# An attention and mixer kernel on one core: the first channel matmul of six groups by Strassen's scheme

## The chip, the core and the metric

The kernel runs on one core of one Trainium2 chip. Its engines run side by side, each with its own instruction queue: TensorE (PE, matrix products, with a separate record PEld for loading the stationary operand), VectorE (DVE), ScalarE (ACT), GpSimd (POOL), and SyncE (SP), which here only issues transfers (DMAs). The metric is the device time of one execution in microseconds (us), lower is better. Matrix products read from on-chip memory (SBUF) and add into banks of a second memory (PSUM), from which DVE and ACT read.

## What is computed

Linear attention on 8 x 8 heads of 576 rows and 64 columns, then an MLP mixer over the tokens and one over the channels, all in float32:

```python
q_s = softmax(q, axis=-1);  k_s = softmax(k, axis=2)
attn = einsum('bhsd,bhde->bhse', q_s, einsum('bhsd,bhse->bhde', k_s, v))
x = attn.transpose(0, 2, 1, 3).reshape(8, 576, 512)
h = relu(x.transpose(0, 2, 1) @ w_tok1) @ w_tok2      # 576 -> 256 -> 576
u = x + h.transpose(0, 2, 1)
out = u + relu(u @ w_ch1) @ w_ch2                     # 512 -> 1536 -> 512
```

The last line is where most of the arithmetic lies: 4608 rows by 512 by 1536, twice. `ch1` is the first of these products with its relu, `ch2` the second.

## The kernel before

**Precision.** A float32 operand is held as two tiles in a reduced float32 (F32R), a high part and the remainder (names ending in h and l; `split`, L108 and L109: ACT copies the high part, DVE or POOL subtracts for the remainder). A product is three matmuls: high by high, remainder of the weights by high, high by remainder of the data.

**Groups and steps.** The 4608 rows of `u`, transposed, are cut into nine groups of 512 columns, kept in three slots `uT[g]`, each of four blocks n of 128 channels. w_ch1 and w_ch2 are cut into twelve rows f of 128. A step (g, f) is `ch1(g, f)`, 4 blocks x 3 = 12 matmuls of 512 columns (L412) into one bank `ps_h`, then relu on ACT (L415, `h2h`) and the remainder on DVE (L416, `h2l`), and `ch2` of the step before (L427): 12 matmuls of 512 columns into four banks `ps_o` that gather over all f. At a group's end `out_end` adds the residual (L459) and sends the group out. The weights of ch1 and ch2 stay in SBUF: `c1h`, `c1l`, `c2`.

**The order.** The list `steps` runs group 0 for f below 4, group 1, the rest of group 0 (24 steps, n0 = 24), and then groups 2 to 8, twelve steps each. Between ch1 and ch2 of a step, functions from the list `todo` are called, which `put(step, function)` has filled: the attention units. A unit is two heads of one batch; batch b is worked on during group b - 1 and gives `uT` of group b (and the end of the group before). Its stages: softmax of q and k (`soft`, DVE, ACT, POOL), `stage_qT` (32x32 transposes on DVE, their copies L331), `stage_kv` (L283), `stage_y` (L345: 14 matmuls of 256 columns), `stage_h1` (L353), `stage_u` (L390), whose result goes to `uT` (L397, L398). `begin` issues the loads of a later unit on SP (`kt` L146, `q` L138, `k` L151; `v` L161 and L162 are issued in `stage_kv`). After the last step of group g POOL computes the residual `u` of its four blocks (`residual`, L442).

**What sets the order on each engine.** The program's order gives priorities; a planner that simulates the engines at compile time lays out each engine's queue (SP's too) by what is ready, and puts in the semaphores. On the chip every queue is then worked off in that order. `behind(...)` ties an instruction behind another on its engine.

**Banks.** `ps_h` has four banks, shared by ch1 and all attention stages from step 0 on; `ps_o` has four, for ch2.

**Weights.** In the first steps `load_ch` loads float64 weights, narrows them on DVE and ACT and splits them; rows 4 to 11 in steps 1 to 11.

Of the kernel before, what the change touches and what calls it, by code (L numbers as in the profile page):

```python
# [20 lines left out]
def attn_mixer_kernel(ctx: ExitStack, tc: tile.TileContext, q, k, kt, v, wt, out, dims):  # L21
# [25 lines left out]
    hpool = ctx.enter_context(tc.tile_pool(name="hpool", bufs=2))  # L47
# [55 lines left out]
    def f32(ap):  # L103
        return ap.bitcast(F32)

    def split(hi, lo, src, lo_eng):

        nc.scalar.copy(hi, src)  # L108
        lo_eng.tensor_tensor(lo, src, f32(hi), op=ALU.subtract)  # L109
# [55 lines left out]
    def load_weights(i, n=CW, out=None):  # L165

        if not wide:
            t = out if out is not None else cv.tile([P, C1 * P], F32, name="cv_s")[:, 0:n]
            nc.sync.dma_start(t, wt[i][:, 0:n])
            return t  # L170
        conv.append(conv.pop(0))
        raw = conv[-1][0].tile([P, CW, 2], U32, name="stg")
        nc.sync.dma_start(raw[:, 0:n, :].rearrange("p n w -> p (n w)"), wt[i][:, 0:n].bitcast(U32))
        with behind(first):
            return narrow(raw, n, out)
# [38 lines left out]
        split(w2h[:, :, S0:S], w2l[:, :, S0:S], t, nc.vector)  # L214

    def load_ch(f):
        h_, l_ = (w[:, f].rearrange("p n m -> p (n m)") for w in (c1h, c1l))
        split(h_, l_, load_weights(AT_C1 + f), nc.vector)
        split(*c2[f], load_weights(AT_C2 + f), nc.vector)

# [145 lines left out]
    uT = [slots[i] for i in (0, 1, 2, 1, 0, 2, 1, 0, 2)]  # L366
# [33 lines left out]


    drained = []

    def ch1(g, f):
        hh = hpool.tile([P, CW], F32R, name="h2h")
        hl = hpool.tile([P, CW], F32R, name="h2l")
        t = ps_h.tile([P, 512], F32, name="ps_h")
        i = 0
        for n in range(NJ):
            uh, ul = (x[:, n, :] for x in uT[g])  # L410
            for a, w in ((c1h, uh), (c1l, uh), (c1h, ul)):
                nc.tensor.matmul(t, a[:, f, n, :], w, start=(i == 0), stop=(i == 3 * NJ - 1))  # L412
                i += 1
        drained[:] = [
            nc.scalar.activation(hh, t, AF.Relu).ins,  # L415
            nc.vector.scalar_tensor_tensor(hl, t, 0.0, f32(hh), op0=ALU.max, op1=ALU.subtract).ins,  # L416
        ]
        return hh, hl

    def ch2(acc, f, first, last, hh, hl, in_turn=False):  # L420

        at = []
        for n, o in enumerate(acc):
            cs = slice(n * P, (n + 1) * P)
            for i, (a, w) in enumerate(((c2[f][0], hh), (c2[f][1], hh), (c2[f][0], hl))):
                with behind(at):
                    m = nc.tensor.matmul(o, a[:, cs], w, start=(first and i == 0), stop=(last and i == 2))  # L427
# [3 lines left out]
    def stage_rows():

        for n in range(0, NJ, 2):
            t = stg.tile([P, CW, 2], U32, name="stg").rearrange("p n w -> p (n w)").bitcast(F32)
            res[n], res[n + 1] = t[:, 0:CW], t[:, CW : 2 * CW]

    def residual(g):

        stage_rows()
        for n in range(NJ):  # L440
            uh, ul = (x[:, n, :] for x in uT[g])
            nc.gpsimd.tensor_tensor(res[n], f32(uh), f32(ul), op=ALU.add)  # L442

    res = {}

    def out_end(g, acc, whole):
        if g == 1:
            stage_rows()
        for n, o in enumerate(acc):
            uh, ul = (f32(x[:, n, :]) for x in uT[g])  # L450
            if g == NG - 1:

                for x, eng in ((slice(0, CW // 2), nc.scalar), (slice(CW // 2, CW), nc.sync)):
                    nc.vector.tensor_tensor(res[n][:, x], o[:, x], res[n][:, x], op=ALU.add)
                    eng.dma_start(out[g, n][:, x], res[n][:, x])
                continue
            if g > 1:
                t = res[n]
                nc.vector.tensor_tensor(t, o, t, op=ALU.add)  # L459
# [94 lines left out]
    steps = [(0, f) for f in range(F_HEAD)] + [(1, f) for f in range(NF)] + [(0, f) for f in range(F_HEAD, NF)]  # L554
    n0 = len(steps)
# [26 lines left out]
    pend = None  # L582

    load_at = dict(zip((1, 2, 4, 5, 7, 8, 10, 11), range(F_HEAD, NF)))
    for i, (g, f) in enumerate(steps):
        if i in load_at:
            if load_at[i] == F_MORE:
                more_pools.close()
                conv[:] = [(stg, cv)]
                c2_rows(F_MORE, NF)  # L590
            with behind(drained):
                load_ch(load_at[i])
        h = ch1(g, f)
# [9 lines left out]
        if pend is None or pend[0] != g:  # L603
            acc = [ps_o.tile([P, CW], F32, name="ps_o") for _ in range(NJ)]
        pend = (g, acc, f, pend is None or pend[0] != g, last, *h)
        if last and g > 1:
            residual(g)
    assert not todo

    ch2(*pend[1:], in_turn=True)  # L610
    out_end(*pend[:2], True)


def pieces(w_tok1, w_tok2, w_ch1, w_ch2):
# [53 lines left out]
```

## Time and profile before

| what | value |
|---|---|
| median of 3 runs | 824.63 us (824.05 to 824.95) |
| profiled execution, first to last instruction (its span) | 822.3 us |
| around the span, against the median | 2.3 us |
| DMA | 63.55 MB, mean 77 GB/s |
| ACT busy | 325.1 us |
| POOL busy | 113.2 us |

The profile is that of one execution. Busy times are sums over the span; a busy PE says that matmuls are in flight. A slice row gives, for each fortieth of the span, a digit that is the busy share in tenths. A stage row gives the busy time of each engine inside a window. A row of a group of instructions has the source line, the engine and operation, output and inputs by the program's names, shapes and count, then the busy time in us and the mean of one in ns, then the time that the engine stood idle before them, and for what.

### The profile page before, as it was taken

How to read it: one execution, taken by the hardware profiler on the slowest of the kernel's cores; microseconds unless marked ns; L12 is line 12 of the kernel's file. 1: busy time of each engine (PE TensorE's matmuls, PEld its weight loads, DVE VectorE, ACT ScalarE, POOL GpSimd, SP SyncE). 2: the span in 40 equal slices, each digit the busy share in tenths (PEclk: the TensorE clock that was granted, in tenths of full speed). 3: DMA queues.
4: the chain of work that ended last, by engine and by line, in shares of the span. 5: the costliest groups of instructions: out<-in, count | busy, mean ns of one | idle time of the engine just before them, and what ended most of it. 6: DMA issues, size and time to landing. Idle time of an engine off the chain costs nothing.

```text
span 822.3 us, 11725 instructions
## 1 busy us (share of the span) xinstructions
PE 796.0 (97%) x4464; PEld 669.9 (81%) x4464; DVE 496.9 (60%) x1080; ACT 325.1 (40%) x758; POOL 113.2 (14%) x93
## 2 busy tenths in 40 slices
PE   3799999999999999999999999999999999999998
PEld 2688888778888888888888888888888888888886
DVE  7999998999775555756657654655566322112112
ACT  4676543466543344434434443444434321111100
POOL 1000000022211011311122011311131102001100
PEclk9999999999999999999999999999999999999999
DMA  8653533424222122322232221322131001001001
GB/s 247 231 143 119 189 118 103 129 69 145 79 61 84 51 63 63 98 63 63 63 114 63 50 60 39 108 63 62 32 98 47 16 1 52 1 0 52 1 1 51
DMA packets 61208, 63.55 MB, mean 77 GB/s; under 512 B 40928, under 2 KB 42080, under 8 KB 61152
## 3 DMA queue, kind: packets, MB, share of 16 engines
q1 hardware_dynamic: 55968, 53.88, 22.3%
q10 hardware_dynamic: 5184, 8.92, 3.0%
q8 instruction: 35, 0.57, 0.3%
q14 instruction: 21, 0.17, 0.1%
HBM read 53.35 MB, written 9.44 MB: 76 GB/s over the span
## 4 chain that ended last, share of the span: by engine, by line
PE 82%; DVE 9%; DMA 4%; ACT 2%; issue 2%; POOL 0%; SPq 0%; ACTq 0%; DVEq 0%; POOLq 0%
PE ps_h L412 32%; PE ps_o L427 32%; PE ps_h L390 7%; PE ps_h L345 5%; PE ps_h L283 2%; DMA q_t<-in_q 2%; PE ps_h L353 1%; DVE q_t L331 1%; PE ps_o L390 1%; PE ps_h L242 1%; DMA out<-stg 1%; DVE h2l L416 1%; DVE st L252 1%; DVE q_t L253 1%; PE ps_o L345 1%
## 5 line engine op out<-in xcount | busy, mean ns | idle before, releaser
L416 DVE SCALAR_TENSOR_TENSOR h2l<-ps_h,h2h 128x512 fp32r<-128x512 f32 x108 | 74.1, 686 | 163.0 <-ACT h2h L415 162.4
L427 PE MATMUL ps_o<-h2h,c2h 128*128 128x512 f32 x432 | 169.2, 392 | 1.2 <-ACT h2h L415 1.2
L412 PE MATMUL ps_h<-uh,c1h 128*128 128x512 f32 x432 | 169.2, 392 | 0.0
L427 PE MATMUL ps_o<-h2h,c2l 128*128 128x512 f32 x432 | 168.8, 391 | 0.0
L412 PE MATMUL ps_h<-uh,c1l 128*128 128x512 f32 x432 | 168.7, 391 | 0.0
L412 PE MATMUL ps_h<-ul,c1h 128*128 128x512 f32 x432 | 168.6, 390 | 0.0
L415 ACT ACTIVATE h2h<-ps_h 128x512 fp32r<-128x512 f32 x108 | 64.5, 597 | 250.8 <-PE ps_h L412 233.0
L427 PE MATMUL ps_o<-h2l,c2h 128*128 128x512 f32 x432 | 152.6, 394 | 0.0
L331 DVE COPY q_t<-cv_s 32x160 f32<-32x160 f32 (+1 forms) x252 | 67.6, 268 | 61.6 <-POOL ql L109 58.5
L427 PEld LDWEIGHTS ps_o<-h2h,c2h 128*128 128x128 f32 x432 | 81.1, 188 | 18.1 <-ACT h2h L415 1.6
L412 PEld LDWEIGHTS ps_h<-ul,c1h 128*128 128x128 f32 x432 | 81.1, 188 | 17.4
L427 PEld LDWEIGHTS ps_o<-h2h,c2l 128*128 128x128 f32 x432 | 81.2, 188 | 16.2
L412 PEld LDWEIGHTS ps_h<-uh,c1h 128*128 128x128 f32 x432 | 81.1, 188 | 15.9
L412 PEld LDWEIGHTS ps_h<-uh,c1l 128*128 128x128 f32 x432 | 81.2, 188 | 15.0
L427 PEld LDWEIGHTS ps_o<-h2l,c2h 128*128 128x128 f32 x432 | 79.6, 188 | 15.8
L244 POOL TENSOR_TENSOR k_t<-k_t,dg 128x640 f32<-128x640 f32 x24 | 38.2, 1592 | 310.4 <-ACT dg L243 296.3
L109 POOL TENSOR_TENSOR ql<-q_t,qh 128x640 fp32r<-128x640 f32 x24 | 37.7, 1569 | 197.4 <-ACT qh L108 161.2
L442 POOL TENSOR_TENSOR stg<-uh,ul 128x512 f32<-128x512 f32 x28 | 35.5, 1290 | 141.3 <-DMA out<-stg 111.8
L252 DVE TENSOR_REDUCE st<-q_t 128x10 f32<-128x640 f32 x32 | 26.1, 816 | 37.0 <-DMA q_t<-in_q 36.8
L262 ACT ACTIVATE q_t<-q_t 128x640 f32<-128x640 f32 x32 | 23.6, 738 | 47.1 <-DVE q_t L253 47.0
L331 ACT COPY q_t<-cv_s 32x128 f32<-32x128 f32 (+1 forms) x132 | 40.6, 307 | 2.9 <-DVE cv_s L321 1.4
L390 PE MATMUL ps_h<-w2h,hh 128*128 128x256 f32 (+1 forms) x112 | 32.9, 301 | 0.1
(144 smaller groups left out, 1152.1 us busy)
## 6 DMA issues: line engine op xcount, KB each, us to landing
stg<-in_w SPq DMA_DIRECT2D x28, 512.0 KB, 3.4
kt_t<-in_kt SPq DMA_DIRECT2D x32, 320.0 KB, 2.9
q_t<-in_q SPq DMA_DIRECT2D x32, 320.0 KB, 2.9
v_t<-in_v SPq DMA_DIRECT2D x64, 128.0 KB, 3.0
k_t<-in_k SPq DMA_DIRECT2D x24, 320.0 KB, 3.5
out<-stg ACTq DMA_DIRECT2D x28, 256.0 KB, 3.4
v_t<-in_v SPq DMA_DIRECT2D x32, 32.0 KB, 2.9
out<-part ACTq DMA_DIRECT2D x4, 256.0 KB, 3.5
```

The costliest lines, as they stand in the source:

```text
L109: lo_eng.tensor_tensor(lo, src, f32(hi), op=ALU.subtract)
L244: nc.gpsimd.tensor_tensor(kx, kx, dg.unsqueeze(1).broadcast_to([P, C1, P]), op=ALU.subtract)
L252: nc.vector.tensor_reduce(st[:, 0, :], qt, axis=AX.X, op=ALU.max)
L262: nc.scalar.activation(qc, qc, AF.Exp)
L331: eng(qx[ys, 0:n, xs], turned[xs, 0:n, ys])
L345: nc.tensor.matmul(y[:, 0:TOK], a, w, start=(i == 0), stop=(i == len(mm) - 1))
L390: nc.tensor.matmul(t[:, 0:N], a, w, start=(i == 0), stop=(i == len(mm) - 1))
L412: nc.tensor.matmul(t, a[:, f, n, :], w, start=(i == 0), stop=(i == 3 * NJ - 1))
L415: nc.scalar.activation(hh, t, AF.Relu).ins,
L416: nc.vector.scalar_tensor_tensor(hl, t, 0.0, f32(hh), op0=ALU.max, op1=ALU.subtract).ins,
L427: m = nc.tensor.matmul(o, a[:, cs], w, start=(first and i == 0), stop=(last and i == 2))
L442: nc.gpsimd.tensor_tensor(res[n], f32(uh), f32(ul), op=ALU.add)
```

## The change

For groups 3 to 8 (from `G_S` = 3) two rows f of ch1 are computed together as a product of 2 x 2 blocks: weights A cut into (two rows f) x (two halves of the 512 channels), data B cut into (two halves of the channels) x (two halves of 256 columns). In the form of Strassen's scheme that uses 7 products, the products are

- P1 = A11 B11, P2 = A12 B21, P3 = (A12 - A21 - A22 + A11) B22, P4 = A22 (B21 - B22 + B12 - B11)
- P5 = (A21 + A22)(B12 - B11), P6 = (A21 + A22 - A11)(B22 - B12 + B11), P7 = (A11 - A21)(B22 - B12)

each of 2 blocks x 3 matmuls of 256 columns. The weight sums are made once per pair of rows (`keep_sums`), split, and written to memory with the plain blocks (`keep_blocks`), in steps 18 to 32. They come back product by product into a ring of eight SBUF tiles of 256 KB (`load_product`, on SP, issued when the tile's former product is done). The ring and the tiles of the data sums take the place of c1's rows, which are in two pools now and are closed in steps 32 and 35. The data sums are made once per group on DVE and split (`data_sums`); they need `u` as one float32 value per element, so the residual is made before the group (`row_sum`), three blocks on POOL and one on DVE. `pair_a` (P1, P6, P5, P7, in the even step) and `pair_b` (P2, P3, P4, in the odd step) join the products in SBUF, then come relu and remainder as before, from SBUF. A pair's two halves go to ch2 one per step, from the step after. Attention units of batches 3 to 7 start one step earlier. Groups 0 to 2 keep the old ch1.

```diff
+    h2 = hpool.tile([P, 2, 2, CW], F32R, name="h2")
     def ch1(g, f):
-        hh = hpool.tile([P, CW], F32R, name="h2h")
-        hl = hpool.tile([P, CW], F32R, name="h2l")
+        hh, hl = (h2[:, x, f % 2, :] for x in range(2))
...
+    def keep_blocks(p):
+        scratch_w[p] = [dpool.tile([P, 2, 2 * P], F32, name=f"w{p}_{i}") for i in range(7)]
+        for e, f, n in ((P1, 2 * p, 0), (P2, 2 * p, 2), (P4, 2 * p + 1, 2)):
+            for x, w in enumerate(c1_row(f)):
+                nc.sync.dma_start(scratch_w[p][e][:, x, :], f32(w[:, n : n + 2, :].rearrange("p n m -> p (n m)")))
+    def keep_sums(p):
...
+        nc.vector.tensor_tensor(a, f32(wh[:, i : i + 2]), f32(wl[:, i : i + 2]), op=ALU.add)
...
+        nc.vector.tensor_tensor(s[:, 0], a21, a22, op=ALU.add)
+        nc.vector.tensor_tensor(s[:, 1], s[:, 0], a11, op=ALU.subtract)
+        nc.vector.tensor_tensor(s[:, 2], a11, a21, op=ALU.subtract)
+        nc.vector.tensor_tensor(s[:, 3], a12, s[:, 1], op=ALU.subtract)
+        split(hi, lo, f32(lo), nc.vector)
+        for k, e in enumerate(sums):
+            for x, w in enumerate((hi, lo)):
+                nc.sync.dma_start(scratch_w[p][e][:, x, :], f32(w)[:, k * 2 * P : (k + 1) * 2 * P])
...
+    def load_product():
...
+            nc.sync.dma_start(f32(ring[i % 8].rearrange("p n m -> p (n m)")), scratch_w[p][e].rearrange("p x m -> p (x m)"))
...
+    def row_sum(g, n, eng):
+        uh, ul = (x[:, n, :] for x in uT[g])
+        eng.tensor_tensor(rows_of(g)[n // 2][:, n % 2, :], f32(uh), f32(ul), op=ALU.add)
...
+    def data_sums(g, which):
...
+        for i in which:
+            o, a, b = ((f0, b12, b11), (f1, b22, f0), (f0, b22, b12), (f0, b21, f1))[i]
+            nc.vector.tensor_tensor(o, a, b, op=sub)
+            split(T[0][:, i], T[1][:, i], tf[i == 1], nc.vector)
...
+    def product(g, e, t, cols):
...
+        for n in range(2):
+            for a, b in ((w[:, n], bh), (w[:, 2 + n], bh), (w[:, n], bl)):
+                nc.tensor.matmul(t[:, cols], a, b[:, n], start=(i == 0), stop=(i == 5))
+                i += 1
+        load_product()
+    def pair_a(g, p):
+        x = ps_h.tile([P, 512], F32, name="ps_h")
+        product(g, P1, x, A)
+        product(g, P6, x, Bq)
+        c = odd[p % 2]
+        c11, both, c22 = c[:, 0:HW], c[:, HW : 3 * HW], c[:, 3 * HW :]
+        nc.scalar.copy(c11, x[:, A])
+        nc.vector.tensor_tensor(c22, x[:, Bq], c11, op=ALU.add)
+        y = ps_h.tile([P, 512], F32, name="ps_h")
+        product(g, P5, y, A)
+        product(g, P7, y, Bq)
+        nc.vector.tensor_tensor(halves(both), halves(y[:, 0:CW]), c22.unsqueeze(1).broadcast_to([P, 2, HW]), op=ALU.add)
+        nc.vector.tensor_tensor(c22, y[:, A], both[:, Bq], op=ALU.add)
+        held[0] = c, c11, both
+    def pair_b(g, p):
+        c, c11, both = held.pop(0)
+        x = ps_h.tile([P, 512], F32, name="ps_h")
+        product(g, P2, x, A)
+        nc.vector.tensor_tensor(c11, x[:, A], c11, op=ALU.add)
+        z = ps_h.tile([P, 512], F32, name="ps_h")
+        product(g, P3, z, A)
+        product(g, P4, z, Bq)
+        nc.vector.tensor_tensor(both, z, both, op=ALU.add)
+        out = []
+        for r in (slice(0, CW), slice(CW, 2 * CW)):
+            hh, hl = h_slots[at_h[0] % 3]
+            at_h[0] += 1
+            nc.scalar.activation(hh, c[:, r], AF.Relu)
+            nc.vector.scalar_tensor_tensor(hl, c[:, r], 0.0, f32(hh), op0=ALU.max, op1=ALU.subtract)
...
-            at = [n0 + (b - 3) * NF + 3 * j + x for x in (0, 1, 1.5, 2)]
+            at = [n0 - 1 + (b - 3) * NF + 3 * j + x for x in (0, 1, 1.5, 2)]
...
+    for p, at in enumerate((18, 21, 24, 27, 29, 31)):
+        put(at, lambda p=p: keep_blocks(p))
+        put(at + 1, lambda p=p: keep_sums(p))
...
+        for n in range(NJ):
+            last_n = g < NG - 1 and n == NJ - 1
+            put(at - 2 if g < NG - 1 and n > 1 else at - 5, lambda g=g, n=n, last_n=last_n: row_sum(g, n, nc.vector if last_n else nc.gpsimd))
+        put(at - 2, lambda g=g: data_sums(g, (0, 1, 2)))
+        put(at - 1, lambda g=g: data_sums(g, (3,)))
+    put(n0 + 8, lambda: stage_pair_pools(0))
+    put(n0 + 9, lambda: [load_product() for _ in range(6)])
+    put(n0 + 11, lambda: stage_pair_pools(F_MORE))
+    put(n0 + 11, lambda: [load_product() for _ in range(2)])
...
-        h = ch1(g, f)
+        more = []
+        if g < G_S:
+            more = [(f, ch1(g, f))]
+        elif f % 2 == 0:
+            pair_a(g, f // 2)
+        else:
+            more = list(zip((f - 1, f), pair_b(g, f // 2)))
...
-        if last and g > 1:
-            residual(g)
```

More of the change, by code (lines that the diff above doesn't have):

```diff
@@ L37, in attn_mixer_kernel @@
     F_HEAD, F_MORE = 4, 8
+    G_S = 3
+    HW = CW // 2
     const = ctx.enter_context(tc.tile_pool(name="const", bufs=1))
@@ L85, in attn_mixer_kernel, with c1_rows, c1_row @@
     const.tile([P, 96], F32, name="shift")
-    c1h = const.tile([P, NF, NJ, P], F32R, name="c1h")
-    c1l = const.tile([P, NF, NJ, P], F32R, name="c1l")
     const.tile([P, 32], F32, name="shift_back")
+    ctx.enter_context(tc.tile_pool(name="edge", bufs=1, side="right")).tile([P, 24], F32, name="edge")
+    c1, c1_pools = {}, {}
+    def c1_rows(f0, f1, side):
+        c1_pools[f0] = ExitStack()
+        pool = c1_pools[f0].enter_context(tc.tile_pool(name=f"c1_{f0}", bufs=1, side=side))
+        t = [pool.tile([P, f1 - f0, NJ, P], F32R, name=f"c1{x}{f0}") for x in "hl"]
+        for f in range(f0, f1):
+            c1[f] = t, f - f0
+    def c1_row(f):
+        t, i = c1[f]
+        return [x[:, i] for x in t]
+    c1_rows(0, F_MORE, "right")
     c2 = {}
@@ L216, in load_ch @@
     def load_ch(f):
-        h_, l_ = (w[:, f].rearrange("p n m -> p (n m)") for w in (c1h, c1l))
+        h_, l_ = (w.rearrange("p n m -> p (n m)") for w in c1_row(f))
         split(h_, l_, load_weights(AT_C1 + f), nc.vector)
@@ L410, in ch1 @@
             uh, ul = (x[:, n, :] for x in uT[g])
-            for a, w in ((c1h, uh), (c1l, uh), (c1h, ul)):
-                nc.tensor.matmul(t, a[:, f, n, :], w, start=(i == 0), stop=(i == 3 * NJ - 1))
+            for a, w in ((wh, uh), (wl, uh), (wh, ul)):
+                nc.tensor.matmul(t, a[:, n, :], w, start=(i == 0), stop=(i == 3 * NJ - 1))
                 i += 1
@@ L418, in ch1, with halves @@
         return hh, hl
+    NP = NF // 2
+    P1, P6, P5, P7, P2, P3, P4 = range(7)
+    sums = [P5, P6, P7, P3]
+    scratch_w = {}
+    def halves(x):
+        return x.rearrange("p (n w) -> p n w", n=2)
+    def keep_blocks(p):
[3 more added lines that the diff above has]
+                nc.sync.dma_start(scratch_w[p][e][:, x, :], f32(w[:, n : n + 2, :].rearrange("p n m -> p (n m)")))
@@ new lines, in attn_mixer_kernel, with rows_of @@
+    loads = [(p, e) for g in range(G_S, NG) for p in range(NP) for e in range(7)]
+    asked = [0]
+    def load_product():
+        i = asked[0]
+        if i < len(loads):
+            p, e = loads[i]
+            nc.sync.dma_start(f32(ring[i % 8].rearrange("p n m -> p (n m)")), scratch_w[p][e].rearrange("p x m -> p (x m)"))
+            asked[0] += 1
+    rows = {}
+    def rows_of(g):
+        if g not in rows:
+            if g % 2:
+                rows[g] = [part[:, n : n + 2, :] for n in (0, 2)]
+            elif g - 2 in rows:
+                rows[g] = rows[g - 2]
+            else:
+                rows[g] = [
+                    stg.tile([P, CW, 2], U32, name="stg").rearrange("p n w -> p (n w)").bitcast(F32).rearrange("p (n w) -> p n w", n=2)
+                    for _ in range(2)
+                ]
+        return rows[g]
@@ new lines, in attn_mixer_kernel @@
+    at_product, at_h = [0], [0]
+    def product(g, e, t, cols):
+        w = ring[at_product[0] % 8]
+        at_product[0] += 1
+        uh, ul = uT[g]
+        k = {P1: (0, A), P2: (2, A), P3: (2, Bq)}
+        if e in k:
+            n, s = k[e]
+            bh, bl = uh[:, n : n + 2, s], ul[:, n : n + 2, s]
+        else:
+            bh, bl = (halves(x[:, {P5: 0, P6: 1, P7: 2, P4: 3}[e]]) for x in T)
+        i = 0
+        for n in range(2):
[3 more added lines that the diff above has]
+        load_product()
@@ new lines, in pair_b @@
+    def pair_b(g, p):
[13 more added lines that the diff above has]
+            nc.vector.scalar_tensor_tensor(hl, c[:, r], 0.0, f32(hh), op0=ALU.max, op1=ALU.subtract)
+            out.append((hh, hl))
+        return out
@@ L429, in ch2 @@
                     at = [m.ins]
[L431 to L444, printed above, removed]
     def out_end(g, acc, whole):
         if g == 1:
-            stage_rows()
+            t = [stg.tile([P, CW, 2], U32, name="stg").rearrange("p n w -> p (n w)").bitcast(F32) for _ in range(2)]
+            res = [x[:, h * CW : (h + 1) * CW] for x in t for h in range(2)]
+        elif g > 1:
+            res = [rows_of(g)[n // 2][:, n % 2, :] for n in range(NJ)]
         for n, o in enumerate(acc):
@@ L602, in attn_mixer_kernel @@
         last = i + 1 == len(steps) or steps[i + 1][0] != g
-        if pend is None or pend[0] != g:
-            acc = [ps_o.tile([P, CW], F32, name="ps_o") for _ in range(NJ)]
-        pend = (g, acc, f, pend is None or pend[0] != g, last, *h)
-        if last and g > 1:
-            residual(g)
+        for ff, h in more:
+            new = i == 0 or (g < G_S and steps[i - 1][0] != g) or (g >= G_S and ff == 0)
+            if new:
+                acc = [ps_o.tile([P, CW], F32, name="ps_o") for _ in range(NJ)]
+            pend.append((g, acc, ff, new, last and ff == more[-1][0], *h))
     assert not todo
-    ch2(*pend[1:], in_turn=True)
-    out_end(*pend[:2], True)
+    now = pend.pop(0)
+    ch2(*now[1:])
+    ch2(*pend[0][1:], in_turn=True)
+    out_end(*pend[0][:2], True)
 def pieces(w_tok1, w_tok2, w_ch1, w_ch2):
```

50 lines of the change are left out of this document (44 added, 6 removed).

## The prediction

> **What bounds the kernel now.** I read the busy table and the slices first, then the busy time by stage, then single rows for prices.
>
> ```profile
> span 822.3 us, 11725 instructions
> ...
> PE 796.0 (97%) x4464; PEld 669.9 (81%) x4464; DVE 496.9 (60%) x1080; ACT 325.1 (40%) x758; POOL 113.2 (14%) x93
> ...
> DVE  7999998999775555756657654655566322112112
> ...
> PEclk9999999999999999999999999999999999999999
> ```
>
> The span is 822.3 us; the median of the runs, 824.63, lies 2.3 us above it, so I add 2.3 to every span below. TensorE (PE) is busy 97% at full granted clock. The question is by stage:
>
> ```profile
> 0.00:110.00 110.00, 90.61 (x602) 77.14 (x603) 101.26 (x233) 64.57 (x147) 2.16 (x17) 0.98 0.58 181
> 110.00:190.00 80.00, 78.11 (x396) 64.35 (x394) 75.15 (x142) 39.57 (x83) 9.18 (x6) 1.00 0.36 116
> 190.00:244.00 54.00, 53.62 (x326) 45.89 (x327) 42.42 (x94) 29.29 (x74) 13.75 (x10) 1.00 0.24 69
> 244.00:333.00 89.00, 89.00 (x520) 75.33 (x519) 51.15 (x118) 36.00 (x85) 10.97 (x7) 1.00 0.23 67
> 333.00:423.00 90.00, 90.00 (x524) 75.91 (x523) 55.23 (x122) 37.11 (x89) 17.96 (x13) 1.00 0.24 70
> ```
>
> Columns: stage, its length, busy PE, weight loads, DVE, ACT, POOL, clock, DMA share, GB/s. Group 2 is 244 to 333, group 3 is 333 to 423; groups 4 to 6 look the same to 690, groups 7 and 8 have no attention work. From group 3 on PE is busy in (nearly) every microsecond and DVE has 39% to spare: the six groups that change are PE's, and PE time taken out of them comes off the end, as long as DVE stays inside its spare time.
>
> **The PE term.** Prices of a 512-column and of a 256-column matmul, from the chain of waits and from the timeline:
>
> ```profile
> 366.90 2.75 PE ps_h L412 x12
> ...
> 772.14 2.72 PE ps_h L412 x12
> 774.86 2.72 PE ps_o L427 x12
> ```
> ```profile
> 380.89 0.28 PE L345 MATMUL ps_h<-w1h,qh 128*128 128x256 f32 x1
> 380.90 0.19 PEld L345 LDWEIGHTS ps_h<-w1l,qh 128*128 128x128 f32 x1
> 381.01 0.28 PE L345 MATMUL ps_h<-w1l,qh 128*128 128x256 f32 x1
> 381.01 0.19 PEld L345 LDWEIGHTS ps_h<-w1h,ql 128*128 128x128 f32 x1
> ...
> 382.57 0.40 PE L427 MATMUL ps_o<-h2h,c2h 128*128 128x512 f32 x1
> ```
>
> One ch1 step is 12 matmuls of 512 columns in 2.72 us (0.227 each); beside attention work it is 2.75. The 14 matmuls of L345, each with weights of its own, go from 380.89 to 382.57: 0.120 us a piece at 256 columns. The two prices fit 0.417 ns a column plus 13 ns a matmul.
>
> A pair of ch1 rows was 24 matmuls of 512: 5.44 us (5.50 beside attention). It becomes 7 products of 2 x 3 matmuls of 256: 42 x 0.120 = 5.04. Saved per pair 0.40, or 0.46 beside attention. Of the 6 x 6 = 36 pairs, 24 (groups 3 to 6) stand beside attention: 24 x 0.46 + 12 x 0.40 = **15.8 us off PE**. At 0.40 throughout it is 14.4.
>
> Here the Trainium skill speaks against the change: "TensorE: Matmul & The Clock Gate", section Back-to-back issue gap, gives a sustained roofline of about 81 ns a matmul at N = 128 and 131 at N = 512 for streams of weight load and matmul. By a straight line between them 256 columns would cost an estimated 98 ns, a pair 4.1 us where it was 3.1, and the kernel would be some 35 us slower. The rows above (0.227 at 512, 0.120 at 256) agree with neither figure, and I sum by the rows.
>
> **What is added on DVE.** Prices:
>
> ```profile
> L416 DVE SCALAR_TENSOR_TENSOR h2l<-ps_h,h2h 128x512 fp32r<-128x512 f32 x108 | 74.1, 686 | 163.0 <-ACT h2h L415 162.4
> ...
> L253 DVE TENSOR_TENSOR q_t<-q_t,st 128x640 f32<-128x640 f32 x32 | 26.2, 821 | 0.7
> ...
> L459 DVE TENSOR_TENSOR stg<-ps_o,stg 128x512 f32<-128x512 f32 x24 | 15.5, 679 | 7.1 <-PE ps_o L427 7.1
> ...
> L347 ACT COPY ys<-ps_h 128x256 f32<-128x256 f32 x29 | 10.6, 366 | 2.0 <-PE ps_h L345 1.9
> ...
> L109 DVE TENSOR_TENSOR c1l<-cv_s,c1h 128x512 fp32r<-128x512 f32 x12 | 8.2, 683 | 0.0
> ...
> L108 ACT CAST c1h<-cv_s 128x512 fp32r<-128x512 f32 x12 | 7.4, 620 | 2.7 <-DVE cv_s L189 2.7
> ...
> L454 DVE TENSOR_TENSOR stg<-ps_o,stg 128x256 f32<-128x256 f32 x8 | 2.8, 418 | 2.1 <-PE ps_o L427 2.1
> ```
>
> Joins of a pair: three of 256 columns (0.42, as L454) and two of 512 (0.68, as L459): 2.6 us. The relu and its remainder (L415, L416) stay, with SBUF as source; no row prices that, I take L416's 0.69 and no difference. ACT gains a 256 copy, 0.37. Per group: joins 6 x 2.6 = 15.6; data sums 4 subtractions and 4 remainders of 512, 8 x 0.68 = 5.4; one of the four row sums, which POOL made, 0.7. Together 21.7 us DVE, and on ACT 6 x 0.37 + 4 x 0.62 = 4.7. In group 3 DVE goes from 55.2 of 90.0 to 76.9 of 87.6: **88%**.
>
> Weight sums, once per pair, in steps 18 to 32: a sum and a remainder of 1024 (1.2 each, from the step 512 to 640 of L109 and L253) and four of 256: 4.1 us DVE, 24 in all, with 1 us ACT and 14 DMAs of 128 KB on SP. Two pairs fall into 190 to 244: DVE 42.4 + 8.2 = 50.6 of 54, 94%; the rest falls into group 2 (79% then).
>
> **What that costs PE.** The stages above are the yardstick: with DVE 79% busy (190 to 244) PE lost 0.38 of 54 us, 0.7%; with DVE 94% busy (110 to 190) 1.89 of 80, 2.4%. At 88% the line between gives 1.7% of the 350 us of groups 3 to 6, 6.0 us, and 0.9 for the front: 7 at most. At least nothing: the order on every engine is laid out at compile time by readiness (below), the pair's halves are needed by ch2 only one ch2 and four products later (2.72 + 2.88 = 5.6 us), and the chain join, relu, remainder is 0.68 + 0.60 + 0.69 plus handing over. I take **4**, as part of the loss at 94% was a wait for weights that these groups don't have. Where joins are late, what is queued behind them on DVE is the attention's softmax and remainders, and PE's y and u stages wait for those; PE runs dry once DVE is some 5 us behind.
>
> **The weights.** 42 loads of 256 KB a group from memory: 11 MB, in 87.6 us 126 GB/s on top of 70, and 176 GB/s where there is no attention. The front ran 181 GB/s at a DMA share of 0.58, so 196 is 0.63. A slot is asked for when its product ends and used again seven products and two ch2 later: 7 x 0.72 + 5.4 = 10.5 us at least, 12 or more beside attention.
>
> ```profile
> kt_t<-in_kt SPq DMA_DIRECT2D x32, 320.0 KB, 2.9
> ...
> out<-stg ACTq DMA_DIRECT2D x28, 256.0 KB, 3.4
> ```
>
> With 3 to 3.5 us to landing this is hidden; if not, all of PE waits behind the product's first weight load. The loads share SP's queue with the attention's:
>
> ```profile
> SPq L138 <- DVE qtl L109: 246.8, 22, 15.7
> ```
> ```profile
> 371.84 0.33 SPq L138 DMA_DIRECT2D q_t<-in_q  x1
> 375.98 0.93 SPq L161 DMA_DIRECT2D v_t<-in_v  x2
> 377.00 0.60 SPq L162 DMA_DIRECT2D v_t<-in_v  x1
> 377.65 0.59 SPq L151 DMA_DIRECT2D k_t<-in_k  x1
> 381.63 0.34 SPq L146 DMA_DIRECT2D kt_t<-in_kt  x1
> 393.96 0.33 SPq L138 DMA_DIRECT2D q_t<-in_q  x1
> ```
>
> SP stood before the q load for 11.2 us a time (246.8 over 22), 15.7 at worst. But the code asks for kt, then q, then k, and the queue has k, kt, q: the planner lays SP out by readiness, so the new loads should go into that gap. Cost taken: 0.
>
> **Moved at no cost.** Attention units start one step earlier (their q, k, kt, v loads with them, ahead of the same SP queue): the same PE work in another place, covered because PE is full on both sides. Row sums move ahead of their group on POOL, which is busy 18 of 90. c1 rows 8 to 11 are now written only after the extra staging closes: 0 to one wait for weights; I take 0, since c2 rows waited there already. At the start of group 3, P6 needs its sums after the last u stage: about 4.5 us of chain under ch2, three products, ch2 and P1 (8.3 us). If that cover goes, it costs its excess once a group.
>
> **Sum.** 822.3 - 15.8 + 4 = 810.5, and 2.3 around it: **813**. With no loss 808.8, with the whole loss and the small saving 824.6 - 14.4 + 7 = 817.
>
> **Rivals.**
>
> *DVE becomes the bound (slower).* DVE's idle time in groups 3 to 6 is made of waits inside the attention's chain:
>
> ```profile
> L331 DVE COPY q_t<-cv_s 32x160 f32<-32x160 f32 (+1 forms) x165 | 47.1, 286 | 48.1 <-POOL ql L109 46.0
> L416 DVE SCALAR_TENSOR_TENSOR h2l<-ps_h,h2h 128x512 fp32r<-128x512 f32 x48 | 32.9, 685 | 47.1 <-ACT h2h L415 46.7
> ```
>
> A group had 34.8 us of it. It stays PE's as long as no more than 87.6 - 76.9 = 10.7 remain, and turns slower than before from 13.1. If half remains (17.4), a group takes 94.3 for 90: +17 over four groups, -5 in the last two: **837**. For it: L331 waits for POOL whatever stands around it. Against: products end all through the unit, so there is always a join to fill with.
>
> *Ring loads stuck behind the q load.* If the planner does put q first and the worst wait (15.7) returns, it exceeds the 12 us cover by some 3.5 us. In three or four of the 16 units that is 10 to 14 us, **823 to 827**. Against it stands the order above.
>
> *Narrow matmuls pay more than L345's.* The change loses once the fixed cost of a matmul is over 85 columns' worth, 36 ns. The narrowest full-array rows come near:
>
> ```profile
> 657.43 0.60 PE L353 MATMUL ps_h<-kvf,ys 128*128 128x128 f32 x4
> ...
> 657.79 0.36 PE L390 MATMUL ps_h<-qth,kvh 128*128 128x256 f32 x1
> ```
>
> Four in 0.36: 90 ns, 37 above their columns. With that, 42 x 0.143 = 6.0 a pair, +0.5 x 36: **843**. The 256-column rows speak against it. The prices of the Trainium skill (the page and section above) would end on this side too.
>
> **Chances.** Forecast (809 to 817) 0.72; the same with DVE lateness worth 8 to 13 us (817 to 822) 0.07; DVE bound 0.12; SP queue 0.07; narrow matmuls 0.02. The range 808.5 to 822.5 leaves out the slower cases, 0.2. About 0.2% (1.6 us) can be told from no change: faster 0.78, same 0.06, slower 0.16.
>
> **What would show it.** Right: in groups 7 and 8 a pair takes 10.5 us for 10.9; product matmuls start 0.12 apart; DVE is near 77 of 87.6 us in group 3; PE's idle time there is under 2%, with DVE tiles (c, h2l) as releasers. Wrong: PE idle before product matmuls on DMA ring loads, SP waits of L138 with ring loads behind them, DVE above 95% with PE below, or product pitch above 0.13.

## The result, and the profile after

The changed kernel takes 830.50 us (median of 20 runs, 827.42 to 833.89); the kernel before, measured beside it, 825.66 (20 runs). The ratio is 1.0058, 95% interval 1.0047 to 1.0070: **slower by 0.6%**, 4.8 us, where 813 was predicted. The profiled execution has a span of 826.1 us, 3.8 more than before (822.3).

From the page of the changed kernel, span, busy table (share of the span, instructions) and DVE's row of the slices:

```profile
span 826.1 us, 14182 instructions
...
PE 784.3 (95%) x5112; PEld 692.0 (84%) x5112; DVE 640.0 (77%) x1349; ACT 352.0 (43%) x824; POOL 112.1 (14%) x88
...
DVE  7899999799889865978788789878797647535433
```

PE is busy for 784.3 us where it was 796.0: 11.7 us of work did leave it. But it idles for 41.8 us (826.1 - 784.3) where it idled for 26.3. The 15.5 us of new idle time pay back the saving and 3.8 more. The stages, columns as in the prediction (stage, length, busy PE, weight loads, DVE, ACT, POOL, clock, DMA share, GB/s), say where:

```profile
110.00:190.00 80.00, 76.46 (x379) 63.11 (x379) 72.12 (x134) 37.62 (x77) 8.62 (x5) 0.98 0.44 137
190.00:244.00 54.00, 49.69 (x297) 42.33 (x296) 48.02 (x107) 30.12 (x75) 8.71 (x5) 1.00 0.44 132
244.00:333.00 89.00, 88.52 (x519) 74.64 (x517) 67.75 (x148) 39.96 (x93) 22.95 (x15) 1.00 0.43 128
333.00:423.00 90.00, 87.82 (x658) 80.33 (x657) 73.56 (x162) 41.06 (x99) 18.32 (x12) 1.00 0.63 198
423.00:690.00 267.00, 258.76 (x1850) 234.98 (x1849) 214.05 (x459) 116.21 (x291) 46.19 (x31) 0.99 0.58 179
690.00:810.00 120.00, 120.00 (x760) 109.00 (x759) 58.08 (x101) 21.11 (x41) 5.18 (x4) 1.00 0.60 189
```

From 110 to 333 us, in groups whose matmuls did not change, PE idles for 8.3 us, before for 2.3. From 333 to 690 (groups 3 to 6) it is 10.4 of 357 us, before 0.74. After 690, without attention, PE is full. DVE is at 82% in group 3, and its busiest stage behind 110 us, up to 190, has 90%, where it had 94% before; the loss is made of single waits. PE's waits from 110 us on (engine, line, waited for: total us, times, longest), after and then before:

```profile
PE ps_h L406 <- DVE hl L377: 7.1, 5, 2.1
PE ps_o L592 <- ACT h L432: 4.0, 3, 3.4
PE ps_h L406 <- DVE c L571: 2.1, 1, 2.1
PE ps_o L592 <- DVE h L433: 1.6, 1, 1.6
PE ps_o L592 <- ACT h3h L580: 1.6, 4, 0.6
PE ps_h L406 <- ACT hh L376: 1.1, 1, 1.1
```
```profile
PE ps_o L427 <- ACT h2h L415: 1.2, 2, 0.7
PE ps_h L390 <- DVE hl L361: 0.6, 1, 0.6
```

These six make 17.5 us, the two largest of before 1.8. The waiting lines are not the products: L406 is the units' u stage (L390 before), L592 is ch2. They wait for hl, the remainder of the units' own relu, for h, and once for a join of the products (c).

Three trains of events make most of it. **At a group's border** DVE has more to do at one time than PE's next stage can wait for. DVE of the changed kernel, start and duration, around 435 us:

```profile
428.90 0.68 DVE L562 TENSOR_TENSOR c<-ps_h,c 128x512 f32<-128x512 f32 x1
429.50 1.61 DVE L125 TENSOR_TENSOR tl<-tf,th 128x512 fp32r<-128x512 f32 x1
...
431.31 0.41 DVE L563 TENSOR_TENSOR c<-ps_h,c 128x256 f32<-128x256 f32 x1
431.65 2.71 DVE L347 COPY q_t<-cv_s 32x160 f32<-32x160 f32 x11
...
434.53 1.82 DVE L612 TENSOR_TENSOR part<-ps_o,part 128x512 f32<-128x512 f32 x3
436.27 0.82 DVE L282 TENSOR_TENSOR q_t<-q_t,st 128x640 f32<-128x640 f32 x1
437.00 0.69 DVE L612 TENSOR_TENSOR part<-ps_o,part 128x512 f32<-128x512 f32 x1
437.60 0.42 DVE L377 SCALAR_TENSOR_TENSOR hl<-ps_h,hh 128x256 fp32r<-128x256 f32 x1
```

DVE goes without a gap: a join (L562), a data sum's remainder, a join (L563), the copies, three of the group's four outputs, softmax, the fourth output, and only then hl. PE resumes when hl is done. Even ACT's half of that relu was late, by 3.08 us, as it is queued behind an output transfer that waits for DVE's L612:

```profile
435.57 0.38 ACT L376 ACTIVATE hh<-ps_h 128x256 fp32r<-128x256 f32 x1 [3.08 <-DVE part L612]
```

**In the front** a load is late. The transfers of the weight blocks run here (SP's queue; duration min/median/max, first and last start; these are the high parts, the 18 of the low parts run beside them), while the code puts them at steps 18 to 31, past 200 us:

```profile
L450 SPq DMA_DIRECT2D w<-c1h x18: 319/342/742, 57.0 to 167.5; - x18
```

Beside them the weight stream's own loads come late. DVE's wait for them between 110 and 190 us, before and after:

```profile
DVE cv_s L182 <- DMA stg<-in_w: 0.9, 1, 0.9
```
```profile
DVE cv_s L198 <- DMA stg<-in_w: 6.1, 7, 1.3
```

L198, a step of narrowing a weight row, feeds ACT's L199, and h (L432) of the next ch1 row is behind L199 in ACT's queue: this is the longest wait of the table, 3.4 us at 163 us. It costs more than itself:

```profile
163.00:167.00 4.00, 0.66 (x12) 0.40 (x6) 2.82 (x6) 1.23 (x3) 0.00 (x0) 0.95 0.82 226
167.00:170.00 3.00, 2.97 (x7) 2.39 (x8) 3.00 (x6) 0.97 (x4) 1.55 (x1) 0.50 0.31 115
```
```profile
167.00:170.00 3.00, 3.00 (x20) 2.65 (x19) 2.99 (x7) 1.54 (x6) 0.00 (x0) 1.00 0.00 0
```

After 4 us with 0.66 of work the granted clock is 0.50 for the next 3 us: PE counts as busy with 7 matmuls where the kernel before (second fence) runs 20. The Trainium skill, "TensorE: Matmul & The Clock Gate", section Why this matters for your kernels, asks for no PE gap above some 3 us, after which the clock falls to half. The trace agrees here.

**Behind it come the weight sums.** DVE makes them from 193 to 284 us (L459 to L464). Two waits of PE lie there, 1.6 us for hl until 220 us and 1.6 us for h (L433) until 233, each with weight sums just ahead of the awaited result in DVE's queue.

### The profile page after: what moved, and what is told of

Its sections match the earlier page's. It is cut to its first block, busy times and chain, and to the rows that moved or that the text cites. A ratio compares the mean times of both kernels' runs of the same rounds, so it can differ in the third digit from the quotient of the medians.

```text
span 826.1 us, 14182 instructions
## 1 busy us (share of the span) xinstructions
PE 784.3 (95%) x5112; PEld 692.0 (84%) x5112; DVE 640.0 (77%) x1349; ACT 352.0 (43%) x824; POOL 112.1 (14%) x88
## 2 busy tenths in 40 slices
DMA packets 109605, 140.78 MB, mean 170 GB/s; under 512 B 46304, under 2 KB 58208, under 8 KB 109536
## 4 chain that ended last, share of the span: by engine, by line
PE 50%; DVE 29%; DMA 12%; ACT 4%; issue 3%; SPq 2%; DVEq 0%; ACTq 0%
PE ps_o L592 20%; PE ps_h L544 15%; PE ps_h L406 5%; DMA q_t<-in_q 5%; DMA stg<-in_w 4%; DVE q_t L347 3%; PE ps_h L429 2%; PE ps_h L361 2%; DVE q_t L282 2%; DVE st L268 1%; DVE h L433 1%; DMA w<-stg 1%; DVE st L279 1%; DVE q_t L269 1%; DVE qtl L125 1%
## 5 line engine op out<-in xcount | busy, mean ns | idle before, releaser
L592 PE MATMUL ps_o<-h,c2h 128*128 128x512 f32 x672 | 225.6, 395 | 5.6 <-ACT h L432 4.0
L592 PEld LDWEIGHTS ps_o<-h,c2h 128*128 128x128 f32 x672 | 125.4, 189 | 30.1 <-ACT h L432 4.6
L592 PE MATMUL ps_o<-h,c2l 128*128 128x512 f32 x336 | 132.4, 394 | 0.0
L544 PE MATMUL ps_h<-th,ring 128*128 128x256 f32 x576 | 107.3, 283 | 0.1
L544 PEld LDWEIGHTS ps_h<-th,ring 128*128 128x128 f32 x576 | 89.7, 192 | 0.4 <-DVE c L575 0.3
L544 PE MATMUL ps_h<-uh,ring 128*128 128x256 f32 x432 | 82.6, 285 | 0.0
L544 PE MATMUL ps_h<-tl,ring 128*128 128x256 f32 x288 | 81.4, 283 | 0.0
L592 PEld LDWEIGHTS ps_o<-h,c2l 128*128 128x128 f32 x336 | 63.8, 190 | 11.4
L347 DVE COPY q_t<-cv_s 32x160 f32<-32x160 f32 (+1 forms) x252 | 59.1, 235 | 14.1 <-POOL ql L125 10.9
L125 POOL TENSOR_TENSOR ql<-q_t,qh 128x640 fp32r<-128x640 f32 x24 | 38.6, 1609 | 214.1 <-ACT qh L124 147.9
L429 PE MATMUL ps_h<-uh,c1h 128*128 128x512 f32 x144 | 56.4, 391 | 0.0
L429 PE MATMUL ps_h<-uh,c1l 128*128 128x512 f32 x144 | 56.3, 391 | 0.0
L429 PE MATMUL ps_h<-ul,c1h 128*128 128x512 f32 x144 | 56.1, 390 | 0.0
L581 DVE SCALAR_TENSOR_TENSOR h<-c,h 128x512 fp32r<-128x512 f32 x48 | 41.9, 890 | 5.9 <-ACT h L580 5.8
```

Of the source, the lines that this page charges most:

```text
L347: eng(qx[ys, 0:n, xs], turned[xs, 0:n, ys])
L429: nc.tensor.matmul(t, a[:, n, :], w, start=(i == 0), stop=(i == 3 * NJ - 1))
L544: nc.tensor.matmul(t[:, cols], a, b[:, n], start=(i == 0), stop=(i == 5))
L581: nc.vector.scalar_tensor_tensor(hl, c[:, r], 0.0, f32(hh), op0=ALU.max, op1=ALU.subtract)
```

## Experiments

Times are medians; the ratio is to the kernel before, run beside it, with its 95% interval. "Against after" compares two such ratios (1 point in the third decimal is 0.8 us), so differences below some 2 us are not read. Theory 1: PE waits for late DVE and ACT work. Theory 2: the new transfers make PE wait. Theory 3: the front loses because the planner draws the weight blocks and sums forward.

### What do the added parts cost, one at a time?

**Ring loaded once.** Eight loads, no more.

```diff
-        if i < len(loads):
+        if i < 8:
```

> The ring is loaded once (8 products) and not again: 244 transfers of 256 KB and their places in SP's queue are gone, all else is the same. Theory 1: 829 to 831, as product matmuls do not wait for the ring now. Theory 2: 818 to 824.

830.06 us, 1.0067 (1.0045 to 1.0089): no difference from after. The profile has 64 MB less to move (76.77 for 140.78 MB), and that is worth nothing; Theory 2 falls for the ring.

**No joins.**

```diff
-        nc.vector.tensor_tensor(c22, x[:, Bq], c11, op=ALU.add)
...
-            nc.scalar.activation(hh, c[:, r], AF.Relu)
+            nc.scalar.activation(hh, z, AF.Relu)
```

> The joins are left out: relu and remainder of both halves read the bank of P3 and P4, DVE loses 2.6 us a pair and ACT the 256 copy; products and transfers are the same. Theory 1: the 8 us of stalls in groups 3 to 6 go, about 822. Theory 2: 830. If the data sums at the group boundaries alone are to blame: 828.

818.84, 0.9923 (0.9898 to 0.9948): 11 us less than after. PE's waits for hl:

```profile
PE ps_h L406 <- DVE hl L377: 2.8, 5, 1.2
```

7.1 us became 2.8, though nothing of the attention was changed: DVE's joins, ahead of hl in its queue, were in the way. The edit takes two things along: ACT's copy goes, and relu and remainder read PSUM in place of SBUF, where none of the 72 remainders took longer than 0.69 us (in the changed kernel nine took 1.49 to 2.10, see the last section). From 333 to 690 us alone, hl went from 5.5 to 1.6 us, and the wait for c (2.1) is gone. So 11 us is the price of the joins with what hangs on them.

**Data sums in one group only.**

```diff
-        for i in which:
+        for i in which if g == G_S else ():
```

> The data sums are made for group 3 alone and used for all six groups: DVE loses 5.4 us and ACT 2.5 at each later group boundary. If the stalls of groups 3 to 6 come from the burst at the boundary (data sums, row sum, out_end and joins together): 6 us fewer, about 824.5. If they come from the joins: 829 to 830.

827.09, 1.0017 (1.0000 to 1.0034): 3.4 us less, between the two expectations. The border wait before 438 us went, those before 528 and 618 us stayed, so the data sums are a part of the border's load, not all of it.

**No weight sums.** The transfers stay, the arithmetic goes.

```diff
-        nc.vector.tensor_tensor(a, f32(wh[:, i : i + 2]), f32(wl[:, i : i + 2]), op=ALU.add)
...
-        split(hi, lo, f32(lo), nc.vector)
+        hi, lo = (x[:, i : i + 2].rearrange("p f n m -> p (f n m)") for x in (wh, wl))
```

> The arithmetic of the weight sums is left out (6 x 4.1 us DVE, 6 x 1 us ACT in steps 18 to 32); the plain blocks are written to memory in their place, so SP's transfers are the same 84. Theory 1 (PE is made to wait by DVE and ACT work that comes late): the 5.4 us of PE stalls between 190 and 255 us go, about 825 where the changed kernel has 830.5. Theory 2 (the transfers in SP's queue make PE wait): 830.

824.36, 0.9984 (0.9966 to 1.0001): 6 us less, as Theory 1 had it. Work that is done once, before the first product, costs some two fifths of the 14.4 us that all products were to save on PE.

### Is it the front?

**Front only.** G_S is set past the last group: no pairs, no data sums, no ring; the weight blocks, their sums and everything else stay.

```diff
-    G_S = 3
+    G_S = NG
```

> No pairs: all groups keep the old ch1. What is left of the change is the weight sums and their transfers, c1 in two pools and the units one step earlier. Theory 1 (the front loses 8 us of PE time by itself): 825.6 + 8 = 833 to 834. If the front's stalls only come with the pairs, or are given back later because PE has spare time there: 826 to 828.

828.32, 1.0035 (1.0021 to 1.0050). That is the second of the two expectations, but without a single product the kernel is already 2.9 us slower than before. DVE waits for the weight loads as in after:

```profile
DVE cv_s L198 <- DMA stg<-in_w: 6.2, 7, 1.8
```

**Sums put at steps 24 to 34**, so that they should fall into group 2.

```diff
-    for p, at in enumerate((18, 21, 24, 27, 29, 31)):
+    for p, at in enumerate((24, 26, 28, 30, 32, 33)):
```

> The weight sums are made in steps 24 to 34 (group 2, where DVE was busy 51 of 89 us) and no longer in steps 18 to 23. Theory 1: the stalls of 5.4 us between 190 and 255 go, 825 to 826 where the changed kernel has 830.5; group 2 then holds 25 us more of DVE work, if that costs as much there, 830.

830.68, 1.0063 (1.0038 to 1.0088): a miss. The sums ran at 197 to 287 us, as in after (193 to 284). Where the code puts work that depends on nothing late does not decide when it runs.

**Products from group 6 on, and from group 7 on**, sums put at 26 to 55.

```diff
-    G_S = 3
+    G_S = 6
...
+    for p, at in enumerate((26, 30, 40, 44, 50, 54)):
```

> Pairs in groups 6 to 8 alone (18 of 36), weight sums spread over groups 2 to 4. PE work saved 18 x 0.40 = 7.2. Theory 1: one boundary stall (1.5) and at most the 3 us near 163 us are left, 821 to 823. If a pair costs PE more than it saves wherever it stands: above 826.

> Pairs in groups 7 and 8 alone (12 of 36), which have no attention work beside them. PE work saved 12 x 0.40 = 4.8, no stalls in those groups. Theory 1: 821 to 824, with 0.40 us gained a pair in the trace. If a pair costs PE more than it saves wherever it stands: above 826.

823.69, 0.9977 (0.9961 to 0.9992), and 823.08, 0.9972 (0.9958 to 0.9985). Two or three groups gain a little; in both the waits of the front remain (3.1 and 2.2 us, until 167 and 221 us, from group 6; 2.5 and 2.2 from group 7).

**The same, tied.** The blocks and the sums are issued behind the latest k load of SP and the latest relu, so that they cannot be drawn forward; from group 7, from group 6, and for the full change with steps 24 to 34.

```diff
+            last_load[:] = [nc.sync.dma_start(t.rearrange("p c d -> p (c d)"), k[n]).ins]
...
+    def tied(fn, p):
+        with behind(last_load + drained):
+            fn(p)
...
+        put(at, lambda p=p: tied(keep_blocks, p))
+        put(at + 1, lambda p=p: tied(keep_sums, p))
```

> As the kernel with pairs in groups 7 and 8 alone, but the transfers and sums of the weights are tied behind the attention's last k load and behind ch1 of their step, in steps 38 to 58, so the planner cannot draw them forward. Theory 3 (the front loses 3 to 5 us because the planner draws the weight blocks' transfers forward to 60 us and the sums to 193 us): the front is that of the kernel before and the whole 4.8 us stays, 820.5 to 821.5. If the front's loss comes from c1 in two pools or the units' shift: 823, as without the tie.

> Pairs in groups 6 to 8 with the same tie, weight sums in steps 38 to 57. 7.2 us of PE work saved, one boundary stall of 1.5 to 2 at group 6: theory 3 gives 820 to 821, no tie gave 823.7.

> The changed kernel (pairs in groups 3 to 8) with the same tie, weight sums in steps 24 to 34. Theory 3: the front's stalls (3 at 163 us, 5.4 at 190 to 255) go, the stalls of groups 3 to 6 (8 us) stay, 822 to 825; if group 2 cannot take 25 us more of DVE work, 827 to 830.

From group 7: **816.14, 0.9900 (0.9885 to 0.9915)**, faster than both kernels. From group 6: 817.46, 0.9916 (0.9903 to 0.9930). The full change: 828.12, 1.0053 (1.0035 to 1.0071), no better than untied. Against the untied run from group 7 the tie with its later steps is worth 7 of 1000, some 6 us, and later steps without a tie had not moved the sums: Theory 3 holds. The gain was larger than expected (820.5 to 821.5 from group 7). The waits of the tied group-7 version, and of the tied full change:

```profile
PE ps_o L591 <- ACT h L433: 1.2, 2, 0.7
PE ps_h L259 <- DVE ul L415: 0.7, 1, 0.7
```
```profile
PE ps_h L407 <- DVE hl L378: 6.7, 7, 2.1
PE ps_o L593 <- ACT h L433: 3.6, 3, 2.1
PE ps_h L545 <- issue: 2.1, 1, 2.1
PE ps_h L545 <- DVE c L576: 2.1, 1, 2.1
...
PE ps_h L545 <- DVE c L572: 1.2, 1, 1.2
```

In the full change there is no room between the last weight load and the first product: late sums (257 to 337 us) meet the first data sums and joins on DVE (three waits of the products' line L545 between 343 and 354 us), and the borders wait as before. The front was won here too, and lost again in group 2: the outputs of group 0, the last ones ahead of group 2, begin at 248.0 us, in after at 255.2, but those of group 2 begin 103.0 us later, in after 87.7. The group-7 version, though, gained 3 us more than 12 pairs at 0.40.

### Where do the other 3 us come from?

**Units one step earlier**, alone, in the kernel before.

```diff
-            at = [n0 + (b - 3) * NF + 3 * j + x for x in (0, 1, 1.5, 2)]
+            at = [n0 - 1 + (b - 3) * NF + 3 * j + x for x in (0, 1, 1.5, 2)]
```

> The kernel before with one edit of the change: the attention units' first steps one earlier (n0 - 1). No pairs, no sums, no transfers. What the traces so far say: in groups 3 to 6 the kernel before spends about 13 us of PE time above the pitch of its matmuls (N/2.4 + 13 ns), the version with the pairs tied into the last two groups 7.7, and these groups have no pairs in either. Theory A, the moved units alone are worth this: 820 to 822 against 824 to 825. Theory B (the prediction's): the same work in another place, nothing: 824 to 825, and the tied version's extra gain comes from somewhere else. It separates what the change gains without Strassen's products.

827.23, 1.0021 (1.0007 to 1.0035): slower, against Theory A. The waits from 333 to 690, and POOL and DVE at one of the four places:

```profile
PE ps_h L390 <- DVE hl L361: 5.4, 4, 1.4
```
```profile
426.73 5.03 POOL L442 TENSOR_TENSOR stg<-uh,ul 128x512 f32<-128x512 f32 x4 [1.91 <-DMA out<-stg]
```
```profile
426.86 5.68 DVE L331 COPY q_t<-cv_s 32x160 f32<-32x160 f32 x7
432.58 0.42 DVE L361 SCALAR_TENSOR_TENSOR hl<-ps_h,hh 128x256 fp32r<-128x256 f32 x1
```

Seven small DVE copies take 5.68 us while POOL makes the row sums, which had waited for the output's transfer to free their buffer. hl comes after them, and PE waits. On the other side PE switches less often between the 128*64 matmuls of the attention and others (38 times for 54 from 244 to 690 us, counted on its timeline), which by their starts is worth 2.7 us: the moved units bring something and lose it to POOL.

**The group-7 version with the units moved back** (n0). The data sums of group 7 are here issued ahead of the last unit's last row, which they read before it is written; the amount of work is the same.

> The tied version of the last two groups (816.1) with the attention units at the steps that the kernel before has (n0). Theory A (the moved units are worth 3 to 5 us): 819 to 821. Theory B (they are worth nothing): 816. With the run beside it this makes a square: units moved or not, the last two groups by seven products or not.

818.66, 0.9910 (0.9889 to 0.9931): neither theory; the move is worth some 1 of 1000 here, inside the intervals.

**Leftovers only**: as in the front-only run, but without weight blocks and sums; then with the units moved back.

```diff
-    for p, at in enumerate((18, 21, 24, 27, 29, 31)):
-        put(at, lambda p=p: keep_blocks(p))
-        put(at + 1, lambda p=p: keep_sums(p))
```

> The changed kernel with its first Strassen group set past the last group and the weight sums and their transfers taken out: no pairs, no sums. What stays is the units one step earlier, c1 in two pools, the two h slots in one tile, and the row sums put at a step. Theory C (these leftovers reorder work enough to give the 2 to 3 us that the tied versions gain beyond 0.40 a pair): 0.997 of before, 822 to 823. Theory D (they give nothing, the moved units cost what they cost alone): 1.001 to 1.003, 826 to 827.

> The same with the attention units back at n0. Theory C: 0.997 of before or below, 821 to 823. Theory D: 1.000, 824 to 826.

819.95, **0.9928** (0.9908 to 0.9947), and 822.91, 0.9968 (0.9955 to 0.9981). What is neither product nor weight sum makes the kernel 5.9 us faster. Theory C holds, and its size is twice what was expected. In the first of the two, at the same place as above, the same seven copies:

```profile
426.85 1.68 DVE L347 COPY q_t<-cv_s 32x160 f32<-32x160 f32 x7
```

**Units earlier and alternating row buffers**, in the kernel before, nothing else.

```diff
-        stage_rows()
+        if g % 2:
+            res.update({n: part[:, n, :] for n in range(NJ)})
+        elif even:
+            res.update(even)
+        else:
+            stage_rows()
+            even.update(res)
```

> The kernel before with two edits of the change and nothing else: the attention units one step earlier, and the row sums of odd groups in the buffer part, so that two sets of rows alternate and POOL need not wait for the output's transfer. The units alone were 1.0021; there four row sums of POOL (5.0 us) fell on seven DVE copies (L331), which took 5.7 us in place of 1.7, and PE waited for DVE's hl. Theory E (POOL's row sums on top of DVE's copies were the loss, the alternating rows take them away): 0.993 of before, 819 to 821. Theory F (the gain of the leftovers is from c1 in two pools or the h tile): 1.001 to 1.003, 826 to 828.

820.39, 0.9937 (0.9923 to 0.9952): Theory E, as expected. Two small edits give nearly all of the leftovers' gain. With two sets of rows POOL adds each row when its u is done, one at a time, and no longer all four on top of DVE's copies:

```profile
432.14 1.28 POOL L448 TENSOR_TENSOR part<-uh,ul 128x512 f32<-128x512 f32 x1 [8.20 <-DVE ul L398]
```

**Sums tied, no pairs.**

```diff
+    for p, at in enumerate((38, 42, 46, 50, 54, 57)):
+        put(at, lambda p=p: tied(keep_blocks, p))
```

> No pairs, but the weight blocks' transfers and the weight sums, tied behind the latest load and matmul as in the two tied versions, steps 38 to 58. Against the front-only run (1.0035), where they are put at 18 to 32 and drawn forward. Theory 3 (the front loses 3 to 5 us because they are drawn forward): within 1 us of the run without any sums. Its rival (the sums cost DVE time wherever they stand): 3 us or more above that run.

872.04, 1.0561 (1.0540 to 1.0582): a miss that tells nothing of the question. As no product needs the sums, the planner put them behind the last matmul (817 to 864 us):

```profile
820.00:830.00 10.00, 0.00 (x0) 0.00 (x0) 4.21 (x7) 2.06 (x2) 0.00 (x0) 0.50 0.32 105
```

PE had ended at 815.5 us, in the leftovers-only run at 815.4, so the tied transfers of the weight blocks, here at 329 to 487 us, cost PE nothing that these two profiles show. What tied sums cost inside the kernel stays without a measurement of its own.

## Why the prediction was wrong

By three runs that differ by one part each (ratios times 824.6 us; with the intervals of two ratios in it, a step is good to some 2 us):

| step from one kernel to the next | us |
|---|---|
| before to leftovers (units, row buffers, c1 pools) | -5.9 |
| leftovers to front only (weight blocks and sums) | +8.8 |
| front only to the full change (36 pairs) | +1.9 |
| sum | +4.8 |

**The PE term was right.** In groups 7 and 8 a pair takes 10.52 us, as forecast (10.5 for 10.9), with products at 0.120 a matmul. Matmuls that start a half pair (three products, then four), and the next pair:

```profile
780.15 0.40 PE L544 MATMUL ps_h<-uh,ring 128*128 128x256 f32 x2
...
785.05 0.40 PE L544 MATMUL ps_h<-uh,ring 128*128 128x256 f32 x2
...
787.93 0.40 PE L592 MATMUL ps_o<-h,c2h 128*128 128x512 f32 x1
```
```profile
790.67 0.40 PE L544 MATMUL ps_h<-uh,ring 128*128 128x256 f32 x2
```

Four products are 787.93 - 785.05 = 2.88 us, 24 matmuls at 0.120. The rival of dearer narrow matmuls falls. So I take 14.4 for the whole (0.40 a pair) and not 15.8; beside attention no run gives the saving of a pair by itself.

**The step that failed most is "What that costs PE": 4, at most 7 us of waits.** With 14.4 us saved, the pairs' net of +1.9 means some 16 us lost in groups 3 to 6 and at their start. The two profiles, of one execution each, say some 13: from the first output of group 2 to that of group 8 it is 477.3 us in the changed kernel (342.9 to 820.2) and 478.9 in the front-only run (342.0 to 820.9), 1.6 gained of 14.4. PE's own idle time from 333 to 690 us is 10.4 of that; the front-only run has none there. Taking the joins out, with what hangs on them, gives back 11.1, the data sums 3.4; without joins the kernel is 9 us faster than the front-only run (0.9923 for 1.0035), so the products would pay if DVE were not in the way. The sign that I had named for a right forecast, PE idle under 2%, failed with 2.4% in group 3 and 3.1% from 423 to 690 us. The yardstick, PE's idle share against DVE's busy share in other stages, could not see this: DVE ended at 82% in group 3, less than the 88% I had put in. What decides in these traces is how much DVE work stands in one place ahead of a result that PE needs at once, and at a group's border the last joins, the data sums, four outputs, the copies and a softmax come together. I had weighed the cover of the joins' own consumers (5.6 us), which nearly held: L592's waits for h3h are 1.6 us. The queue behind them, which I named, is where it broke: 5.5 us for hl in these groups, 2.1 for a join (c), 1.1 for hh. The rival on DVE had the right engine and the wrong shape: DVE is the bound for a few us at a border, and over no whole stage.

**The second failed step is the price of the weight sums and blocks**, 0.9 us of waits and nothing for the transfers, because they "fall into" 190 to 333 us. They cost 8.8. I had myself noted that the order is laid out by readiness, and used it only where it helped: the blocks are ready as soon as the weights are, so their transfers ran from 57 us on among the weight loads. Here the rival of transfers stuck in SP's queue was right in kind, in another place: the q load's wait shrank,

```profile
SPq L154 <- DVE qtl L125: 43.6, 13, 11.6
```

(it was 246.8, 22, 15.7), and the ring loads were free, as summed. It was the weight stream that had no slack. 6 of the 8.8 go with the arithmetic on DVE (no weight sums against after).

**"Moved at no cost" was wrong in both directions.** Units and row sums together gain some 5 us, by fewer switches on PE and by POOL's rows leaving DVE's copies; the units alone lose 1.7. I had read that the copies wait for POOL, and not that they run slower beside it.

**DVE's prices were low where POOL works.** The relu's remainder from SBUF, for which no row stood, I took at 0.69:

```profile
L581 DVE SCALAR_TENSOR_TENSOR h<-c,h x48: 666/686/2095, 351.0 to 815.5; 128x512 fp32r<-128x512 f32 x48
```

The median is that; the mean is 0.89 and the longest 2.10, for the reason told below. The data sums' remainders (24 of L125), priced at 0.68, have a mean of 0.92. These are part of the 16 us; the run without joins took the first of them out too, and no run separates them from the joins.

Open: what the tied sums cost inside the kernel, and whether it is they that let the tied group-7 version beat the leftovers by only 2.3 us where its 12 pairs save 4.8 (2.5 us less, not much more than the two intervals). Joins laid out by hand against the border were not tried.

## What to carry to other kernels

Where one engine is full, price an edit on another engine by the longest run of its work ahead of a result that the full engine needs at once, not by its busy share. Work without a late dependency is drawn forward to where its inputs are ready: if it must not meet a busy stage, give it a dependency there (the tie was worth 6 us). And take a large edit apart: here the bookkeeping around the products was worth 5.9 us and all the products nothing (1.9 us the wrong way, good to some 2), and the best of these kernels (816.14) is the one that keeps the bookkeeping and uses the products only in the last two groups, where DVE is free.

## What the runs showed of the hardware

Some DVE operations that begin while a POOL operation runs take longer by nearly the rest of it. POOL and DVE of the changed kernel:

```profile
499.40 1.58 POOL L125 TENSOR_TENSOR ql<-q_t,qh 128x640 fp32r<-128x640 f32 x1 [3.75 <-issue]
```
```profile
499.43 2.09 DVE L581 SCALAR_TENSOR_TENSOR h<-c,h 128x512 fp32r<-128x512 f32 x1
```

The remainder started 0.03 us after POOL's op and took 2.09 us for 0.69: 1.4 us longer, nearly POOL's whole duration. Of the 72 remainders at L581 nine took 1.49 to 2.10 us, and each of them began 0.03 to 0.35 us behind the start of a POOL operation; none of the others took longer than 0.69. The same subtraction with one operand in PSUM (L416 before) never took longer than 0.69 in 108 times, though five of them began while a POOL operation ran. Copies from SBUF to SBUF suffer too, as the seven in 5.68 us show that took 1.68 elsewhere. The Trainium skill, "GPSIMD Engine Reference", section 1. Specifications, states that GpSimd shares its SBUF interfaces with VectorE and contends with instructions that have two SBUF inputs or run in a two-port mode; the trace agrees for the subtraction, and for the copies if they run in such a mode, which no run here shows. So a join that reads PSUM is worth keeping, and a POOL op that "runs beside" DVE is not free.

The clock fell after a shorter gap too: a wait of 2.06 us for hl ended at 528.25 us, and the 4 us from 527 on were granted 0.68 (the 4 us behind the wait 0.57).

```profile
527.00:531.00 4.00, 2.75 (x12) 2.76 (x13) 3.73 (x8) 1.61 (x4) 0.87 (x1) 0.68 1.00 368
```

The length of the gap does not settle it: after a wait of 2.08 us that ended at 348.82 us in the same execution, and after one of 2.33 us at 531.06 us in the run with data sums in one group only, the clock stayed at 1.00 for the next 4 us. What tells them apart no run here shows.
